# Batch 0 of an attention and mixer kernel: query and key sums, a convolution tap, u's low parts and two weight loads change engine or place

## The chip, the cores and the metric

The kernel runs on one core of one Trainium2 chip. A core has five engines with queues of their own: TensorE (PE; its weight loads are listed as PEld), VectorE (DVE), ScalarE (ACT), GpSimd (POOL) and SyncE (SP), which issues the transfers here. The metric is device microseconds of one execution.

## The reference

Four batches of 576 positions by 512 channels go through three blocks, all in f32. Only what matters here is shown:

```python
# attention, 8 heads of 64
q_d, k_d, v_d = q, k, v averaged over 4 neighbouring positions
out_up = np.repeat(sm_attn(q_d, k_d, v_d), 4, axis=2)
mask = np.abs(pos[:, None] - pos[None, :]) < 4
x = out_up + softmax(np.where(mask, scale * q @ k.T, -1e9)) @ v
# gated block: a causal depthwise convolution of 5 taps sets the gate
gate = sigmoid(sum over k of conv_w[k] * xp[:, k:k + S, :])
x = (gate * (x @ w_val)) @ w_out
# mixer: over the positions, then over the channels
u = x + (relu(x.T @ w_tok1) @ w_tok2).T
out = u + relu(u @ w_ch1) @ w_ch2
```

## The kernel before

**The attention** (`attention`, a generator per batch) treats two heads at a time, so a batch has four head pairs. For one pair, `load` brings q and k (`qk_sb`), the rows of v in groups of four (`v4_sb`) and v's windows (`v_sb`). `sums` adds groups of four of q and k into `qk_d` (line 266, a DVE reduction; for the first pair of batch 0 four accumulating PE products with a unit matrix, line 263, and an ACT copy, line 264) and groups of v on GpSimd into `vd` (lines 268, 269). `low_scores` makes the averaged scores `sc_d` (line 279) and `loc_scores` those of the band, `sc_l` (lines 319, 325). `softmax` takes maxima on DVE (line 228), exponentials on ACT (line 234) into `e_d` or `e_l`, a reciprocal on DVE (line 238) and the scaling on GpSimd (line 239). `low_turn`, `loc_turn`, `low_out` and `loc_out` transpose these and multiply with v. The averaged part is written into x by ACT (line 309) and the band's part added by DVE (line 360, "the addition" below). `conv` makes the gate from x on DVE: the first tap (line 364) is a multiplication by a scalar, the other four (line 367) multiply and add. Batch 0 takes pair i's scores two steps ahead of pair i-2's outputs.

**The weights** come as 64-bit words. `decode` turns a piece of 256 columns into f32 with three DVE instructions (lines 124, 125, 127, tile `wa`), and splits it into a high part (ACT, line 130) and a low part (GpSimd, line 131). All large products are then three PE products: high by high, high by low, low by high (lines 194 to 196). The data they meet are split alike by `hi_lo` (line 438 on ACT, line 439 on DVE or GpSimd).

**The products of a batch** (`p1`): `p_val` from x, times the gate into `y` (line 476); `p_x`, y by w_out, copied to `u_sb` (line 489); transposes of u (`x2_ps`, split in lines 499 and 500); `r_ps`, the first product over positions, and `p_h`, the second, which is added to u (line 553) and split into `u_hl` (line 554 calls `hi_lo`). `c1` multiplies `u_hl` with w_ch1 (`g_ps`), and `c2` the result with w_ch2 (`p_o`).

**The order.** Batch 0's attention comes first, its steps mixed with eight steps of loading w_val and w_out (two pieces each) and with products of zeros ("fillers", `idle_ps`, line 108). After that PE's order is the written one: `mix` runs the products of the batches one after the other and, at the places that `T_AT` (weights over positions) and `A_AT` (attention of batches 1 to 3) give in a running count of PE time, steps of other generators between them. The other engines are ordered by the framework's scheduler.

```python
T_AT = (2, 14)
A_AT = {1: (0, 57), 2: (59, 136), 3: (138, 216)}
...
    busy(NW0)
    mix((1 for _ in a[0]), [(w, 8, V0, V1), ((busy(NW1) for _ in range(21)), 21, 0, 21)])
```

Buffers that come up below: weights in 64 bits and `wa` have three each, `w_hl` (w_ch1's pieces) four, `v4` one.

Of the kernel before, what the change touches and what calls it, by code (L numbers as in the profile page):

```python
# [14 lines left out]
AF = mybir.ActivationFunctionType  # L15
ALU = mybir.AluOpType
# [18 lines left out]
TAPS = 5  # L35
# [1 line left out]
NW = 16  # L37
LAG = 2
NE = 4
T_AT = (2, 14)  # L40
C2_AT = 285
NM = 2
NW1R = 4
# [9 lines left out]
NW0, NW1 = 8, 3  # L53
# [12 lines left out]
NWD = 3  # L66
NX2 = 4
V0, V1 = 2, 22
A_AT = {1: (0, 57), 2: (59, 136), 3: (138, 216)}
W2_AT = (262, 312)  # L70
NEG = -8.0e9

# [2 lines left out]
def kernel(ctx, tc, qk, vw, v4, w_val, conv_w, w_out, w_tok1, w_tok2, w_ch1, w_ch2, out):  # L75
    nc = tc.nc
# [5 lines left out]
    def T(p, shape, dt, tag, bufs, name=None):  # L82
        return p.tile(shape, dt, tag=tag, bufs=bufs, name=name or tag)
# [15 lines left out]
    cw = T(sb, [128, KC, TAPS], F32, "cw", 1)  # L99
# [5 lines left out]
    def busy(n):  # L105
        for _ in range(n):
            p = T(ps, [128, 512], F32, "ao", BANKS["ao"], name="idle_ps")
            nc.tensor.matmul(p, lhsT=idle[:, 0:128], rhs=idle, start=True, stop=True)
# [93 lines left out]
    def load(b, hp):  # L202

        early = b == 0 and hp > 1
        t = T(sb, [128, 2, PADW], F32, "uhl" if early else "qk", NUH if early else 2, name="qk_sb")
        nc.sync.dma_start(out=t, in_=qk[b, hp])
        tag, bufs = ("x2r", NX2) if b == 0 and hp > 0 else ("v4", NV4)
        w = T(sb, [72, 4, 2, 128], F32, tag, bufs, name="v4_sb")
        nc.sync.dma_start(out=w, in_=v4[b, hp])
        return {"qk": t, "v4": w, "v": load_v(b, hp) if b == 0 else None}  # L210

    def load_v(b, hp):
        tag, bufs = ("w1", NW1R) if b == 0 and hp > 1 else ("v", NV)
        v = T(sb, [128, NCK // 2, 128], F32, tag, bufs, name="v_sb")
        nc.sync.dma_start(out=v, in_=vw[b, hp])
        return v
# [24 lines left out]
    def attention(b):  # L241
# [5 lines left out]
        def bank(shape, name):  # L247
            if b:
                tag = "as" if name[:2] == "sc" else "ao"
            else:  # L250
                tag = TAG0.get(name, "ao")
            return T(ps, shape, F32, tag, BANKS[tag], name=name)

        def sums(hp):
            d = hpd[hp]
            w = d.pop("v4")
            qk_d = T(sb, [128, 2, SD], F32, "qkd", ND, name="qk_d")
            qd, kd = qk_d[:, 0], qk_d[:, 1]
            qk_4 = d["qk"][:, :, 3:3 + S].rearrange("p i (a r) -> p i a r", r=4)
            if b + hp == 0:  # L260
                p = bank([128, 2, SD], "qk_d")
                for r in range(4):
                    nc.tensor.matmul(p, lhsT=ident, rhs=qk_4[:, :, :, r], start=(r == 0), stop=(r == 3))
                nc.scalar.activation(out=qk_d, in_=p, func=AF.Copy)
            else:
                nc.vector.tensor_reduce(out=qk_d, in_=qk_4, axis=AX.X, op=ALU.add)
            vd = d["vd"] = T(sb, [72, 2, 128], F32, "vd", NVD, name="vd")
            nc.gpsimd.tensor_tensor(out=w[:, 0:2], in0=w[:, 0:2], in1=w[:, 2:4], op=ALU.add)
            nc.gpsimd.tensor_tensor(out=vd, in0=w[:, 0], in1=w[:, 1], op=ALU.add)
            d["qkd"] = qd, kd  # L270

        def low_scores(hp):
            d = hpd[hp]
            qd, kd = d.pop("qkd")
            parts = [bank([72, 2, SD], "sc_d") for _ in range(2)]
            for c in range(2):
                for h, p in enumerate(parts):
                    r0 = 64 * h
                    nc.tensor.matmul(p[:, c, :], lhsT=qd[r0:r0 + 64, c * HD:c * HD + HD],
                                     rhs=kd[r0:r0 + 64, :], start=True, stop=True)  # L280
            e = d["ed"] = T(sb, [72, 4, SD], F32, "e", NE, name="e_d")
            softmax(parts, e, 0.125 / 16.0)
# [29 lines left out]
        def loc_scores(hp):  # L312
            d = hpd[hp]
            qk = d.pop("qk")
            parts = []
            for c0, c1 in LU:
                n = c1 - c0
                p = bank([128, n, WIN], "sc_l")
                nc.tensor.matmul(p.rearrange("p a w -> p (a w)"), lhsT=ident16,
                                 rhs=mask[:, c0:c1, :].rearrange("p a w -> p (a w)"), start=True, stop=False)  # L320
                for c in range(n):
                    o = CQ * (c0 + c)
                    for h in range(2):
                        r0 = 64 * h
                        nc.tensor.matmul(p[r0:r0 + 64, c, :], lhsT=qk[r0:r0 + 64, 0, 3 + o:3 + o + WIN],  # L325
                                         rhs=qk[r0:r0 + 64, 1, o:o + WIN], start=False, stop=(c == n - 1))
                parts.append(p)
            e = d["el"] = T(sb, [128, NCK, WIN], F32, "e", NE, name="e_l")
            softmax(parts, e, 0.125)
# [31 lines left out]

        def conv(hp, s0=0, s1=S):
            x, g = x_t[hp], g_t[hp]
            nc.vector.tensor_scalar(g[:, s0:s1], x[:, s0:s1], cw[:, hp, TAPS - 1:TAPS], None, ALU.mult)
            for sh in range(1, TAPS):
                k, t0 = TAPS - 1 - sh, max(s0, sh)
                nc.vector.scalar_tensor_tensor(out=g[:, t0:s1], in0=x[:, t0 - sh:s1 - sh], scalar=cw[:, hp, k:k + 1],  # L367
                                               in1=g[:, t0:s1], op0=ALU.mult, op1=ALU.add)
# [38 lines left out]
        for hp in range(NHP + L):  # L407
            if hp < NHP:
                if hp == 0:
                    for i in range(NHP):  # L410
                        hpd[i] = load(b, i)
                sums(hp)
                low_scores(hp)
                yield
                loc_scores(hp)
                yield
            if hp >= L:
                low_turn(hp - L)
                low_out(hp - L)
                yield  # L420
                loc_turn(hp - L)
                loc_out(hp - L)
                yield
                if hp == NHP + L - 1:
                    conv(hp - L, 0, HS)
                    sigmoid(0, HS)
                    conv(hp - L, HS, S)
                else:
                    conv(hp - L)
                yield  # L430
# [6 lines left out]
    def hi_lo(src_ap, hi_ap, lo_ap, lo_eng):  # L437
        nc.scalar.activation(out=hi_ap, in_=src_ap, func=AF.Copy)  # L438
        lo_eng.tensor_tensor(out=lo_ap, in0=src_ap, in1=hi_ap.bitcast(F32), op=ALU.subtract)  # L439
# [5 lines left out]
    def hv(hs):  # L445
        return slice(hs * HS, hs * HS + HS)
# [11 lines left out]
    def p1(b):  # L458
# [43 lines left out]
        x = x_pair(0)  # L502
# [4 lines left out]
        x = x_pair(1)  # L507
# [35 lines left out]
        us = []  # L543
        for hs in range(2):
            us.append(pair("u", "uhl", NUH))
            for c in range(KC):
                p = bank(P1T["p_h"], "p_h")
                for m in range(2):
                    mm3(p[:, 0:HS], [r[m][:, j, c * 128:c * 128 + 128] for j in range(2)],
                        [t2[m][j][:, hv(hs)] for j in range(2)], m == 0, m == 1)  # L550
                uu = u[:, c, hv(hs)]
                with first():
                    nc.vector.tensor_tensor(out=uu, in0=p[:, 0:HS], in1=uu, op=ALU.add)
                hi_lo(uu, us[hs][0][:, c], us[hs][1][:, c], nc.vector)
                if c == KC - 1:
                    c0 = b * S + hs * HS
                    nc.sync.dma_start(out=u_dr[:, :, c0:c0 + HS], in_=u[:, :, hv(hs)])
                    if hs:
                        u_hl[b] = us
                yield 6 * MM  # L560
# [86 lines left out]
    def mix(main_g, side):  # L647

        now, done = 0.0, [0] * len(side)
        for us in main_g:  # L650
            now += us
            for j, (g, n, t0, t1) in enumerate(side):
                want = n if now >= t1 else max(0, int((now - t0) * n / (t1 - t0)))
                while done[j] < want:
                    done[j] += 1
                    next(g, None)
        for g, _, _, _ in side:
            run(g)

    decode(conv_w, KC * TAPS, 128, None, None, full=cw.rearrange("p c k -> p (c k)"))  # L660
    a = [attention(b) for b in range(B)]
    w = chain(w_sq("val", w_val), w_sq("out", w_out))
    busy(NW0)
    mix((1 for _ in a[0]), [(w, 8, V0, V1), ((busy(NW1) for _ in range(21)), 21, 0, 21)])
    side = [(chain(w_t1(), w_t2()), 7, *T_AT)]
    side += [(a[b], NA, *A_AT[b]) for b in range(1, B)]
    last = c2()
# [47 lines left out]
```

## Time and profile before

| | |
|---|---|
| median of 3 runs | 672.69 us (669.57 to 675.57) |
| profiled execution | 671.3 us, of which the span is 669.5 us |
| busy in the span: PE, PEld | 617.8 us (92%), 531.7 us |
| DVE, ACT, POOL | 351.2 us (52%), 313.1 us, 185.6 us |
| mean granted TensorE clock | 0.956 of full speed |

The times of the runs cover the whole execution; the profiled span begins with its first instruction on an engine. Busy shares are means over the span, whose beginning and end differ much; the rows below therefore cut it into stretches.

### The profile page before, as it was taken

The page shows a single profiled execution, that of the slowest core. Times are in us where ns is not written, and L with a number is a line of the kernel's source. Part 1 is how long each engine was busy: PE and PEld are TensorE (multiplying, and loading weights), DVE is VectorE, ACT ScalarE, POOL GpSimd, SP SyncE. Part 2 cuts the span into 40 slices and gives each one's busy share as a digit, 9 for nine tenths or more (in the row PEclk, how much of TensorE's full clock was granted, in tenths as well). Part 3 has the DMA queues.
Part 4 walks back from the last instruction along what each step waited for, and adds up shares of the span by engine and source line. Part 5 has one row for each costly group of instructions (what it writes and reads, how often), then busy time and mean ns, then how long its engine had stood idle before and what let it go on. Part 6 is the DMA issues. An engine that isn't in the chain of part 4 may idle for free.

```text
span 669.5 us, 12775 instructions
## 1 busy us (share of the span) xinstructions
PE 617.8 (92%) x4884; PEld 531.7 (79%) x4887; DVE 351.2 (52%) x670; ACT 313.1 (47%) x1036; POOL 185.6 (28%) x210
## 2 busy tenths in 40 slices
PE   8898749779879999999999999999998999999996
PEld 4544639658778988899898999998997888888886
DVE  3889997866684456643343644107625232323232
ACT  2785357456537666645656753324433222222221
POOL 5856453431536422223331103303422000000000
PEclk9797859798898999999999999999999999999999
DMA  8634146542675344684332486565997354554220
GB/s 272 207 100 127 56 131 182 158 154 93 207 258 164 118 137 137 195 253 151 101 88 70 135 239 207 163 194 188 309 324 247 95 159 157 156 160 126 79 76 33
DMA packets 53901, 107.23 MB, mean 160 GB/s; under 512 B 5776, under 2 KB 21392, under 8 KB 53840
## 3 DMA queue, kind: packets, MB, share of 16 engines
q1 hardware_dynamic: 53840, 106.42, 51.1%
q8 instruction: 38, 0.62, 0.4%
q14 instruction: 23, 0.19, 0.1%
HBM read 76.52 MB, written 29.88 MB: 159 GB/s over the span
## 4 chain that ended last, share of the span: by engine, by line
PE 59%; DVE 6%; DMA 5%; ACT 3%; issue 2%; POOL 1%; SPq 0%; DVEq 0%; ACTq 0%; POOLq 0%
PE p_o L194 7%; PE p_o L196 7%; PE p_o L195 7%; PE g_ps L194 5%; PE g_ps L195 4%; PE g_ps L196 4%; DMA w<-in_w_ch_dram 4%; PE p_x L194 2%; PE sc_l L325 2%; PE p_val L194 2%; PE p_val L195 2%; PE p_val L196 2%; PE p_x L196 2%; PE p_x L195 2%; PE r_ps L194 1%
## 5 line engine op out<-in xcount | busy, mean ns | idle before, releaser
L194 PE MATMUL g_ps<-u_hl,w_hl 128*128 128x288 f32 x384 | 117.1, 305 | 1.7 <-ACT u_hl L438 1.7
L195 PE MATMUL g_ps<-u_hl,w_hl 128*128 128x288 f32 x384 | 113.9, 297 | 0.3 <-DVE u_hl L439 0.2
L196 PE MATMUL g_ps<-u_hl,w_hl 128*128 128x288 f32 x384 | 113.3, 295 | 0.0
L194 PE MATMUL p_o<-g_hl,ch 128*128 128x512 f32 (+1 forms) x240 | 89.3, 372 | 1.9 <-ACT r_sb L580 1.9
L439 DVE TENSOR_TENSOR g_hl<-r_back,g_hl 128x512 fp32r<-128x512 f32 (+1 forms) x60 | 39.4, 656 | 96.8 <-ACT g_hl L438 91.1
L195 PE MATMUL p_o<-g_hl,ch 128*128 128x512 f32 (+1 forms) x240 | 89.1, 371 | 0.0
L196 PE MATMUL p_o<-g_hl,ch 128*128 128x512 f32 (+1 forms) x240 | 89.1, 371 | 0.0
L438 ACT ACTIVATE g_hl<-r_back 128x512 fp32r<-128x512 f32 (+1 forms) x60 | 35.3, 589 | 110.7 <-PE p_o L196 108.3
L194 PEld LDWEIGHTS g_ps<-u_hl,w_hl 128*128 128x128 f32 x384 | 72.6, 189 | 4.9 <-ACT u_hl L438 1.9
L195 PEld LDWEIGHTS g_ps<-u_hl,w_hl 128*128 128x128 f32 x384 | 72.7, 189 | 0.7 <-DVE u_hl L439 0.7
L196 PEld LDWEIGHTS g_ps<-u_hl,w_hl 128*128 128x128 f32 x384 | 72.7, 189 | 0.0
L367 DVE SCALAR_TENSOR_TENSOR gate_sb<-x_f,cw,gate_sb 128x575 f32<-128x575 f32 (+5 forms) x68 | 60.9, 900 | 0.8
L580 ACT ACTIVATE r_sb<-g_ps 128x288 f32<-128x288 f32 x96 | 38.4, 406 | 48.0 <-PE g_ps L196 40.3
L124 DVE TENSOR_SCALAR wa<-w 128x256 int32<-128x256 int32 (+2 forms) x76 | 39.3, 524 | 35.3 <-DMA w<-in_w_ch_dram 23.7
L194 PEld LDWEIGHTS p_o<-g_hl,ch 128*128 128x128 f32 x240 | 45.2, 188 | 10.9 <-ACT r_sb L580 2.7
L196 PEld LDWEIGHTS p_o<-g_hl,ch 128*128 128x128 f32 x240 | 45.2, 188 | 8.3
L195 PEld LDWEIGHTS p_o<-g_hl,ch 128*128 128x128 f32 x240 | 45.2, 188 | 8.2
L234 ACT ACTIVATE e_l<-sc_l,mx 128x64 f32<-128x64 f32 x160 | 48.2, 334 | 0.4
L194 PE MATMUL p_val<-x_hl,val_hi 128*128 128x288 f32 x128 | 40.7, 318 | 5.8 <-DVE y L476 4.4
L194 PE MATMUL p_x<-y_hl,out_hi 128*128 128x288 f32 x128 | 41.5, 325 | 2.3 <-ACT u_sb L489 1.6
L195 PE MATMUL p_x<-y_hl,out_hi 128*128 128x288 f32 x128 | 39.6, 309 | 2.9 <-DVE y_hl L439 2.8
L439 POOL TENSOR_TENSOR x_hl<-x_f,x_hl 128x288 fp32r<-128x288 f32 x32 | 26.2, 830 | 54.3 <-ACT x_hl L438 54.3
(107 smaller groups left out, 1347.4 us busy)
## 6 DMA issues: line engine op xcount, KB each, us to landing
w_hl<-w_dr SPq DMA_DIRECT2D x36, 512.0 KB
r_dr<-r_sb SPq DMA_DIRECT2D x48, 288.0 KB
w<-in_w_ch_dram SPq DMA_DIRECT2D x48, 256.0 KB
r_back<-r_dr SPq DMA_DIRECT2D x48, 256.0 KB
qk_sb<-in_qk_dram SPq DMA_DIRECT2D x16, 589.0 KB
w_dr<-w_hl SPq DMA_DIRECT2D x12, 512.0 KB
v_sb<-in_vw_dram SPq DMA_DIRECT2D x16, 320.0 KB
v_sb<-in_v_dram SPq DMA_DIRECT2D x16, 288.0 KB
```

The source lines that it names most:

```text
L124: nc.vector.tensor_scalar(a, high, 3, 0x3FFFFFF8, ALU.logical_shift_left, ALU.bitwise_and)
L194: nc.tensor.matmul(out_ap, lhsT=lh, rhs=rh, start=first, stop=False)
L195: nc.tensor.matmul(out_ap, lhsT=lh, rhs=rl, start=False, stop=False)
L196: nc.tensor.matmul(out_ap, lhsT=ll, rhs=rh, start=False, stop=last)
L234: nc.scalar.activation(out=e[:, o, :], in_=p[:, c, :], func=AF.Exp, scale=scale, bias=mx[:, o:o + 1], accum_out=sm[:, o:o + 1])
L325: nc.tensor.matmul(p[r0:r0 + 64, c, :], lhsT=qk[r0:r0 + 64, 0, 3 + o:3 + o + WIN], rhs=qk[r0:r0 + 64, 1, o:o + WIN], start=False, stop=(c ...
L367: nc.vector.scalar_tensor_tensor(out=g[:, t0:s1], in0=x[:, t0 - sh:s1 - sh], scalar=cw[:, hp, k:k + 1], in1=g[:, t0:s1], op0=ALU.mult, op1 ...
L438: nc.scalar.activation(out=hi_ap, in_=src_ap, func=AF.Copy)
L439: lo_eng.tensor_tensor(out=lo_ap, in0=src_ap, in1=hi_ap.bitcast(F32), op=ALU.subtract)
L580: nc.scalar.activation(out=r[:, hv(hs)], in_=p[:, 0:HS], func=AF.Relu)
```

## The change

In batch 0, the sums of q and k of all four pairs are made as the first pair's are (PE products and an ACT copy). The first tap of batch 0's convolution is made by ACT. Batch 0's generator stops once after two of its four pairs' loads, and two steps (four pieces) of w_val are issued there; the other six steps stay in the mix. The low part of u is made by GpSimd in all batches. Two places in the running count change: the weights over positions end later, and batch 1's attention runs from 8 to 59 in place of 0 to 57.

```diff
-T_AT = (2, 14)
+T_AT = (2, 20)
...
-A_AT = {1: (0, 57), 2: (59, 136), 3: (138, 216)}
+A_AT = {1: (8, 59), 2: (59, 136), 3: (138, 216)}
...
-            if b + hp == 0:
+            if b == 0:
                 p = bank([128, 2, SD], "qk_d")
...
-            nc.vector.tensor_scalar(g[:, s0:s1], x[:, s0:s1], cw[:, hp, TAPS - 1:TAPS], None, ALU.mult)
+            if b:
+                nc.vector.tensor_scalar(g[:, s0:s1], x[:, s0:s1], cw[:, hp, TAPS - 1:TAPS], None, ALU.mult)
+            else:
+                nc.scalar.activation(out=g[:, s0:s1], in_=x[:, s0:s1], func=AF.Copy, scale=cw[:, hp, TAPS - 1:TAPS])
...
                         hpd[i] = load(b, i)
+                        if i == 1:
+                            yield
...
-                hi_lo(uu, us[hs][0][:, c], us[hs][1][:, c], nc.vector)
+                hi_lo(uu, us[hs][0][:, c], us[hs][1][:, c], nc.gpsimd)
...
-    mix((1 for _ in a[0]), [(w, 8, V0, V1), ((busy(NW1) for _ in range(21)), 21, 0, 21)])
+    next(a[0])
+    for _ in range(2):
+        next(w)
+    mix((1 for _ in a[0]), [(w, 6, V0, V1), ((busy(NW1) for _ in range(21)), 21, 0, 21)])
```

The first place is DVE's start in batch 0. `sc_l` and `sc_d` are the scores, `mx` their maxima, `qk_d` the sums. Before:

```order
L266 TENSOR_REDUCE qk_d<-qk_sb 128x288
L228 TENSOR_REDUCE mx<-sc_l 128x6
L228 TENSOR_REDUCE mx<-sc_d 72x2 x2
L228 TENSOR_REDUCE mx<-sc_l 128x4
L266 TENSOR_REDUCE qk_d<-qk_sb 128x288
```

After the change, DVE at the same place (`wa` and `w_138`, `w_146`, `w_156` are three pieces of w_val):

```order
L124 TENSOR_SCALAR wa<-w_138 128x256
L125 SCALAR_TENSOR_TENSOR wa<-w_138,wa 128x256
L127 SCALAR_TENSOR_TENSOR wa<-w_138,wa 128x256
L124 TENSOR_SCALAR wa<-w_146 128x256
L125 SCALAR_TENSOR_TENSOR wa<-w_146,wa 128x256
L124 TENSOR_SCALAR wa<-w_156 128x256
L127 SCALAR_TENSOR_TENSOR wa<-w_146,wa 128x256
L125 SCALAR_TENSOR_TENSOR wa<-w_156,wa 128x256
L228 TENSOR_REDUCE mx<-sc_l 128x6
```

Eight instructions on weights now stand ahead of the first maximum, and the sums are gone from the queue.

The second place is PE's written order where batch 1's first head pair has given its scores, among the products of batch 0. Before (`out3` and `out0` are parts of w_out):

```order
L319 MATMUL sc_l_1137<-mask_70,ident16_68 128x256
L325 MATMUL sc_l_1137<-qk_sb_1004 64x64 x8
L279 MATMUL sc_d_1177<-qk_d_1170 72x144
L279 MATMUL sc_d_1178<-qk_d_1170 72x144
L279 MATMUL sc_d_1177<-qk_d_1170 72x144
L279 MATMUL sc_d_1178<-qk_d_1170 72x144
L194 MATMUL p_x2_1095<-y_hl_961,out3_hi_930 128x288
```

After the change, from the same scores on (the `p_val` group has twelve such rows, three for each of four parts of w_val, and `sc_d` follows behind them):

```order
L319 MATMUL sc_l_1214<-mask_70,ident16_68 128x256
L325 MATMUL sc_l_1214<-qk_sb_1136 64x64 x8
L501 MATMUL x2_ps_1243<-ident_63,u_sb_966 128x128 x4
L194 MATMUL p_val_1251<-x_hl_1055,val0_hi_136 128x288
L195 MATMUL p_val_1251<-x_hl_1055,val0_hi_136 128x288
L196 MATMUL p_val_1251<-x_hl_1055,val0_lo_137 128x288
```

Four transposes and twelve products now stand between one pair's band scores and the next pair's averaged scores, which stood back to back before.

The third place is GpSimd's queue while batch 1's `p_h` runs; `e_d`, `e_l`, `v4_sb` and `vd` belong to the attention of batch 3. Before:

```order
L239 TENSOR_TENSOR e_d_3257<-e_d_3257,sm_3259 72x576
L269 TENSOR_TENSOR vd_3853<-v4_sb_3813 72x256
L239 TENSOR_TENSOR e_l_3359<-e_l_3359,sm_3361 128x640
L268 TENSOR_TENSOR v4_sb_3981<-v4_sb_3981 72x512
L439 TENSOR_TENSOR x_hl_3776<-x_f32_2427,x_hl_3776 128x288
```

After the change:

```order
L444 TENSOR_TENSOR u_hl_3314<-u_sb_2395,u_hl_3314 128x288 x2
L239 TENSOR_TENSOR e_d_3272<-e_d_3272,sm_3274 72x576
L269 TENSOR_TENSOR vd_3868<-v4_sb_3828 72x256
L444 TENSOR_TENSOR u_hl_3314<-u_sb_2395,u_hl_3314 128x288 x2
L239 TENSOR_TENSOR e_l_3374<-e_l_3374,sm_3376 128x640
L444 TENSOR_TENSOR u_hl_3436<-u_sb_2395,u_hl_3436 128x288 x2
L268 TENSOR_TENSOR v4_sb_3996<-v4_sb_3996 72x512
L444 TENSOR_TENSOR u_hl_3436<-u_sb_2395,u_hl_3436 128x288 x2
```

The eight low parts of u stand between the attention's instructions, the last two behind the sum of `v4_sb` (line 268).

## Rows read from the trace of the kernel before

**Rows 1.** Stretches: us, busy PE, PEld, DVE, ACT, POOL (instructions), clock, DMA share, GB/s.

```profile
9.94:20.00 10.06, 10.00 (x102) 5.61 (x101) 6.88 (x11) 5.99 (x37) 5.31 (x6) 1.00 1.03 313
20.00:38.56 18.56, 16.15 (x158) 9.66 (x158) 16.55 (x36) 14.06 (x75) 13.30 (x12) 0.72 0.49 170
38.56:71.42 32.86, 26.82 (x259) 14.77 (x261) 30.01 (x51) 18.62 (x67) 21.73 (x22) 0.89 0.37 109
71.42:116.27 44.85, 32.63 (x303) 29.15 (x302) 39.81 (x89) 26.91 (x107) 19.01 (x24) 0.77 0.42 124
116.27:163.94 47.67, 37.22 (x314) 30.92 (x309) 34.99 (x66) 24.84 (x78) 13.81 (x15) 0.86 0.42 129
163.94:205.29 41.35, 34.24 (x305) 31.53 (x303) 29.14 (x59) 19.67 (x66) 17.36 (x20) 0.92 0.72 240
205.29:669.50 464.21, 453.12 (x3442) 406.54 (x3442) 192.40 (x358) 201.77 (x607) 89.14 (x98) 1.00 0.51 158
```

**Rows 2.** PE's waits, 71.42 to 205.29 us: total us, times, longest.

```profile
PE sc_l L319 <- ACT e_d L234: 7.5, 2, 5.8
PE sc_d L279 <- ACT e_l L234: 6.4, 2, 5.9
PE p_val L194 <- DVE y L476: 4.4, 1, 4.4
PE r_ps L195 <- DVE x_hl L500: 2.8, 1, 2.8
```

**Rows 3.** DVE's groups by shape, 0 to 205.29 us: busy us, mean ns, idle before.

```profile
L124 DVE TENSOR_SCALAR wa<-w 128x256 int32<-128x256 int32 x46 | 28.4, 627 | 12.7 <-POOL w_hl L131 7.7 <-DMA w<-in_w_ch_dram 2.8 <-POOL val_lo L131 1.3
L125 DVE SCALAR_TENSOR_TENSOR wa<-w,wa 128x256 int32<-128x256 int32 x46 | 25.1, 556 | 0.3
L127 DVE SCALAR_TENSOR_TENSOR wa<-w,wa 128x256 int32<-128x256 int32 x46 | 21.9, 485 | 0.3
L266 DVE TENSOR_REDUCE qk_d<-qk_sb 128x288 f32<-128x1152 f32 x9 | 12.1, 1348 | 11.4 <-DMA qk_sb<-in_qk_dram 11.4
L439 DVE TENSOR_TENSOR u_hl<-u_sb,u_hl 128x288 fp32r<-128x288 f32 x8 | 4.4, 566 | 3.6 <-ACT u_hl L438 3.6
L364 DVE TENSOR_SCALAR gate_sb<-x_f,cw 128x576 f32<-128x576 f32 x7 | 4.1, 579 | 0.0
L364 DVE TENSOR_SCALAR gate_sb<-x_f,cw 128x288 f32<-128x288 f32 x2 | 0.6, 357 | 0.0
```

**Rows 4.** PE's sums of the first head pair, the same view.

```profile
L263 PE MATMUL qk_d<-qk_sb,ident 128*128 128x288 f32 x8 | 4.4, 704 | 1.2 <-DMA qk_sb<-in_qk_dram 1.2
```

**Rows 5.** ACT's copies into x, the same view.

```profile
L309 ACT ACTIVATE x_f<-o_d 128x576 f32<-128x576 f32 x8 | 5.2, 656 | 3.6 <-PE o_d L306 3.5
```

**Rows 6.** Transfers of one head pair: KB each.

```profile
qk_sb<-in_qk_dram SPq DMA_DIRECT2D x16, 589.0 KB
v_sb<-in_vw_dram SPq DMA_DIRECT2D x16, 320.0 KB
v_sb<-in_v_dram SPq DMA_DIRECT2D x16, 288.0 KB
```

**Rows 7.** DVE in time: start, us, instruction, idle before and its releaser.

```profile
12.43 0.56 DVE L228 TENSOR_REDUCE mx<-sc_l 128x6 f32<-128x384 f32 x1 [1.14 <-PE sc_l L325]
...
21.03 1.31 DVE L124 TENSOR_SCALAR wa<-w 128x256 int32<-128x256 int32 x1 [0.57 <-DMA w<-in_w_val_dram]
...
38.56 0.83 DVE L360 TENSOR_TENSOR x_f<-o_l,x_f 128x290 f32<-128x290 f32 x2 [0.50 <-PE o_l L354]
...
68.33 0.81 DVE L360 TENSOR_TENSOR x_f<-o_l,x_f 128x290 f32<-128x290 f32 x2
```

**Rows 8.** GpSimd's low parts of x by shape, whole span.

```profile
L439 POOL TENSOR_TENSOR x_hl<-x_f,x_hl 128x288 fp32r<-128x288 f32 x32 | 26.2, 830 | 54.3 <-ACT x_hl L438 54.3
```

**Rows 9.** GpSimd while batch 1's p_h runs, in time.

```profile
280.65 1.28 POOL L268 TENSOR_TENSOR v_sb<-v_sb 72x512 f32<-72x512 f32 x1 [0.20 <-DMA v_sb<-in_v_dram]
```

**Rows 10.** One slow instruction of DVE, and GpSimd's scaling beside it, in time.

```profile
119.20 2.90 DVE L124 TENSOR_SCALAR wa<-w 128x256 int32<-128x256 int32 x1 [0.89 <-DMA w<-in_w_ch_dram]
120.68 1.26 POOL L239 TENSOR_TENSOR e_l<-e_l,sm 128x640 f32<-128x640 f32 x1
```

## The prediction

> **What bounds the kernel now.** I read the stretches first [rows 1]. Behind 205.3 us PE is busy 453.1 of 464.2 us at full clock: only PE's own work counts there, and the change leaves that as it is. What can be won lies ahead. PE stands idle for 44.9 - 32.6 = 12.2 us between 71.4 and 116.3, for 10.5 in the next stretch and for 7.1 in the one behind, and its granted clock in these is 0.77, 0.86 and 0.92, so that a part of each passed at 1.2 in place of 2.4 GHz. DVE is the busiest engine of the first two but for PE: 39.8 of 44.9 us and 35.0 of 47.7. Up to 71.4 us batch 0's attention and the weights share DVE and ACT; PE also runs the products of zeros there, so that its busy share says little of need.
>
> Then PE's waits [rows 2]: 5.8 us for the exponentials of `e_d` and 5.9 for those of `e_l`, both of batch 1's first pairs; 2.8 for DVE's split of the transposes, 4.4 for `y`. The releaser of the two long ones is ACT, but ACT waits for maxima, and those stand in DVE's queue among pieces of weights, as DVE's load shows. I read what ends last in these stretches as DVE's backlog.
>
> The sum is made against the profiled execution, 671.3 us (a span of 669.5 and 1.8 around it); the median of the runs, 672.7, is 1.4 us above.
>
> **Stage 1, to 71.4 us.** Removed from DVE: three sums of 1.348 us, 4.0 us, and the first taps, 3 x 0.579 + 2 x 0.357 = 2.5 us [rows 3]. They go to PE, where one pair's sums took 4.4 us [rows 4], 13.2 us for three, and to ACT as three copies and five taps. ACT's price for these isn't in the trace; a copy into x of twice a copy's size took 0.66 us [rows 5], so eight cost at most 5.3. From 9.9 to 71.4 us ACT was busy 38.7 of 61.5 us and PE 53.0 [rows 1], an idle time of 22.8 and of 8.5: on ACT the work has room, on PE part of it has.
>
> Some weights come earlier. The loads of two pairs, 2 x 1.197 MB [rows 6], no longer stand ahead of the first piece; at 313 GB/s [rows 1] that is 7.6 us, so the piece that DVE began at 21.03 [rows 7] comes at about 13.4. Eight instructions on weights now stand ahead of the first maximum: three of 0.627, three of 0.556 and two of 0.485 us [rows 3], 4.5 us. The maximum that began at 12.43 [rows 7] begins at some 17.9, 5.5 us later, and batch 0's chain of scores, exponentials and outputs hangs on it. Against that stand the 4.0 us of sums that DVE no longer makes on the way to the first addition. I count half, since ACT and PE are in that chain too: the first addition moves from 38.56 [rows 7] by 5.5 - 2.0 = 3.5 us. Bounds: 0, if all relief tells and the weights that are done early are missing from the queue later; 8, if the two later pairs arrive late as well.
>
> From the first addition to the last (68.33 [rows 7]) DVE gets one and a quarter pieces more, at 0.627 + 0.556 + 0.485 = 1.67 us 2.1 us, and two sums of batch 1, 2.7, that stood ahead before, less three taps, 1.7: 3.1 us more. DVE was idle for 2.9 us from 38.6 to 71.4 [rows 1], which I let take half: 1.6. The stage ends 5.1 us later, within 0 and 9. **+5**.
>
> **Stage 2, to 116.3 us.** Here the earlier weights pay. By the last addition DVE has done the rest of w_out and much of the first weights over positions, about six pieces more than before: 6 x 1.67 = 10.0 us that leave its 39.8. PE's order now also has four transposes and twelve products between the first pair's band scores and the next `sc_d`. The next stretch has 314 of PE's instructions in 37.2 us [rows 1], 0.12 each, so they cover some 1.9 us of the 5.9 us wait. Cover and relief together I let take the two long waits from 11.8 to 6.8 us: a gain of 5. The clock of 0.77 means that nearly half of the stretch passed at the lower level; with PE standing still less I let it come to 0.87, what the next stretch has: 32.6 x (1 - 0.77/0.87) = 3.8 us. Least: the cover and half the relief's share, 4. Most: all 12.2 us of idle time and a little clock, 13. **-9**.
>
> **Stage 3, to 163.9 us.** The low parts of u leave DVE, 8 x 0.566 = 4.5 us [rows 3], and five pieces of w_ch1 are already done, 8.4 us; DVE's 35.0 us [rows 1] become 22. The wait for the split of the transposes, 2.8 [rows 2], and others like it lose their ground; of 10.5 us of idle time I leave 5, a gain of 5.5. With the clock from 0.86 to 0.92 (the stretch behind) there are 37.2 x (1 - 0.86/0.92) = 2.4 us more. On GpSimd a low part of this size took 0.83 us [rows 8] against DVE's 0.57: the last of eight is ready 0.3 us later. Least 3 (half the waits), most 13 (all of both). **-8**.
>
> **Stage 4, to 205.3 us.** PE's 4.4 us for `y` [rows 2] stand at the end of a stretch in which DVE decodes w_ch1, makes batch 1's convolutions and waits for buffers: 7.7 us of `wa`'s idle time went to GpSimd's low parts of `w_hl` [rows 3]. None of that is removed, and pieces that are done earlier also hold their four buffers earlier. **0**, within -4 and 4.
>
> **Stage 5.** Batches 1 to 3 give 24 more low parts to GpSimd, 19.9 us on an engine that is busy 89.1 of 464.2 us [rows 1, 8]. But its queue is one. In batch 1 the last two low parts stand behind the sum of `v4_sb`, which began at 280.65, when its transfer had come [rows 9], and which itself waits on low parts now; behind it the two end at 281.9 + 2 x 0.83 = 283.6, later by what the transfer is late. They would hold `g_ps` of batch 1 by little or nothing. **+1**, within 0 and 4; there is no gain, since PE is busy all along.
>
> **The sum** is 5 - 9 - 8 + 0 + 1 = -11: 660.3 us against the profiled 671.3, 661.7 on the scale of the median. I predict 661.
>
> **A rule that speaks against the change.** One instruction of line 124 took 2.90 us at 119.20 where the group's mean is 0.63, and lies over GpSimd's scaling of `e_l`, 120.68 to 121.94 [rows 3, 10]. The Trainium skill (SBUF — State Buffer, "Who interferes with whom") says that GpSimd reading SBUF and a DVE instruction that has two inputs there, or that runs in a mode with two ports, lock each other out for a whole instruction. By that rule each low part that moves to GpSimd can hold up a DVE instruction; the trace agrees in this pair of rows. What it would give here is rival D.
>
> **The rivals.**
>
> (B) DVE bounds to 163.9 us as before. For it: DVE is busy 89% and 73% of stages 2 and 3 [rows 1], and w_ch1's pieces wait in line, so that each gap may be filled with the next piece while the maxima wait as now. Then only what is removed counts, 4.0 + 2.5 + 4.5 = 11 us, of which I let 8 reach the end, less the 5 of the later start: -3, 668, or 669 on the median's scale. Against it: PE's order gives cover that doesn't depend on DVE.
>
> (D) The low parts on GpSimd block DVE. In stage 3 eight of 0.83 us [rows 8] hold up 6.6 us of an engine that is needed for the additions to u: -11 + 6.6, 667, or 668. For it speaks the 2.90 us [rows 10]; against it that DVE has little else to do there once five pieces are gone.
>
> (C) Slower: PE becomes the bound of stage 1. Its queue is in order, and the sums of three pairs stand in it among the scores and outputs of the pairs before. From 20 to 38.6 us its clock was 0.72 [rows 1]. At the lower level three sums take 3 x 8.8 = 26.4 us; less the 8.5 us in which PE was idle that is 17.9, without it 26.4. Such a delay of all that follows gives 661.7 + 17.9 = 680, up to 688. The point from which it decides: a stage 1 that ends over 16 us later (5 and the 11 that the forecast gains) is slower than before. Against it: the stage's products of zeros need no result, and the first sums ran at clock 1.00 or near it [rows 1, 4].
>
> **How the numbers follow.** The forecast has 0.60: 0.54 of it faster by over 1%, which is about what a measurement of this kernel can tell from no change (below 666.0 us), 0.06 within. B has 0.18 (0.05 and 0.13), D 0.10 (0.03 and 0.07), C 0.12 (0.10 slower, 0.02 within). Together: faster 0.62, same 0.28, slower 0.10. The half-widths of the terms, 4.5, 4.5, 5, 4 and 2, make 9 us if they are independent of each other; the clock, which is in two of them, joins their low ends, so the range reaches 13 below: low 648. Above, it takes in B and D and ends short of C: high 676.
>
> **What would show it.** Right: the first maximum at 17 to 18 us; batch 0's last addition at 72 to 75; behind it no wait of PE over 4.5 us for `e_d` or `e_l`; the first `g_ps` at about 152 in place of 163.9; and from there to the end the same time. Stage 1 is wrong if the last addition comes at 80 or later, with PE's sums ahead of what it waits for. B would show the same two waits of nearly 6 us, D decoding instructions of over 1.5 us beside `u_hl` on GpSimd, a wrong stage 5 waits of `g_ps` for GpSimd's `u_hl`. What I can't see is where the clock falls next: if it falls as often as now, its 6 us are lost and the time is 667.

## The result, and the profile after

The changed kernel takes 665.73 us (median of 11 runs, 664.11 to 668.48) against 672.21 us of the kernel before beside it: a ratio of 0.9904, 95% interval 0.9879 to 0.9928. That is 6.5 us faster, where 11 were forecast. The profiled execution took 664.67 us (span 662.8) against 671.3 (669.5), 6.6 less.

The stretches of the kernel after answer to [rows 1]. They are cut at the same events: the first addition, the point from which `p_val` runs steadily, the end of batch 0's `p_val` (115.60 us in the kernel before, in place of the 116.27 of [rows 1]), the first `g_ps`, the end of batch 1's first 48 `p_val` (207.03 before). Columns as in [rows 1].

```profile
20.00:45.17 25.17, 23.07 (x196) 10.92 (x194) 15.93 (x36) 18.60 (x104) 16.07 (x17) 1.00 0.62 195
45.17:80.08 34.91, 29.82 (x284) 16.28 (x282) 32.84 (x55) 21.69 (x75) 19.40 (x21) 0.90 0.33 93
80.08:113.32 33.24, 26.47 (x209) 23.35 (x209) 31.66 (x75) 20.52 (x77) 15.71 (x18) 0.95 0.45 140
113.32:151.11 37.79, 35.12 (x353) 30.02 (x352) 29.62 (x53) 23.93 (x89) 15.32 (x16) 0.91 0.49 153
151.11:201.20 50.09, 40.63 (x368) 36.57 (x367) 33.47 (x64) 26.97 (x83) 26.18 (x29) 0.86 0.58 195
201.20:662.80 461.60, 449.50 (x3431) 404.74 (x3429) 185.90 (x332) 200.02 (x605) 105.25 (x121) 1.00 0.51 160
```

The same stretches of the kernel before, cut at its events:

```profile
71.42:115.60 44.18, 31.96 (x267) 28.55 (x267) 39.36 (x88) 26.25 (x105) 18.67 (x23) 0.77 0.41 122
115.60:163.94 48.34, 37.89 (x349) 31.53 (x349) 35.45 (x66) 25.50 (x81) 14.15 (x15) 0.86 0.43 131
163.94:207.03 43.09, 35.98 (x318) 33.27 (x317) 29.96 (x60) 20.84 (x68) 18.73 (x22) 0.92 0.71 237
207.03:669.50 462.47, 451.38 (x3431) 404.80 (x3429) 191.59 (x356) 200.60 (x605) 87.77 (x97) 1.00 0.51 158
```

| stage | before | after | difference | forecast |
|---|---|---|---|---|
| 1, to steady `p_val` | 71.42 | 80.08 | +8.7 | +5 |
| 2 | 44.18 | 33.24 | -10.9 | -9 |
| 3 | 48.34 | 37.79 | -10.6 | -8 |
| 4 | 43.09 | 50.09 | +7.0 | 0 |
| 5 | 462.47 | 461.60 | -0.9 | +1 |

Up to the first `g_ps` 12.8 us are won, and 7.0 of them are gone 50 us later; most of these 7.0 are products that stood before the first `g_ps` and now stand behind it, as shown below. PE's waits from 140 to 215 us after the change, which answer to [rows 2] (total, times, longest):

```profile
PE o_l L354 <- ACT pts_l L343: 3.6, 1, 3.6
PE sc_l L319 <- ACT e_d L234: 2.6, 1, 2.6
PE g_ps L195 <- POOL u_hl L444: 1.6, 3, 0.8
```

The 4.4 us for `y` are no longer there. A wait of 3.6 us for ACT's copies of the transposes stands in their place. In stages 2 and 3 the two waits of nearly 6 us are gone. From 80.08 to 151.11 us these are left of them (the longest anywhere is now the 2.6 above, in stage 4):

```profile
PE sc_l L319 <- ACT e_d L234: 2.2, 1, 2.2
PE sc_d L279 <- ACT e_l L234: 1.0, 1, 1.0
```

DVE in time, for [rows 7] (start, us, idle before):

```profile
16.19 0.55 DVE L228 TENSOR_REDUCE mx<-sc_l 128x6 f32<-128x384 f32 x1
...
45.17 0.83 DVE L360 TENSOR_TENSOR x_f<-o_l,x_f 128x290 f32<-128x290 f32 x2 [2.69 <-PE o_l L354]
...
77.01 0.81 DVE L360 TENSOR_TENSOR x_f<-o_l,x_f 128x290 f32<-128x290 f32 x2
```

The first maximum is 3.8 us later than before, the first addition 6.6 and the last 8.7. Each of these times is from one execution. sig_before, a kernel below whose edit leaves batch 0 alone, has the first addition at 41.16 and the last at 73.70 in its one profile (of the slowest of its runs), 2.6 and 5.4 us later than the kernel before. So differences of a few us in batch 0 count here only where several kernels agree.

### The profile page after: what moved, and what is told of

It reads as the page before. It is cut to its first block, busy times and chain, and to the rows that moved or that the text cites. A ratio compares the mean times of both kernels' runs of the same rounds, so it can differ in the third digit from the quotient of the medians.

```text
span 662.8 us, 12825 instructions
## 1 busy us (share of the span) xinstructions
PE 622.3 (94%) x4911; PEld 529.6 (80%) x4911; DVE 339.4 (51%) x630; ACT 316.4 (48%) x1044; POOL 210.0 (32%) x242
## 4 chain that ended last, share of the span: by engine, by line
PE 60%; DVE 6%; DMA 5%; ACT 3%; issue 2%; POOL 1%; SPq 0%; DVEq 0%; ACTq 0%
PE p_o L194 7%; PE p_o L196 7%; PE p_o L195 7%; PE g_ps L194 5%; PE g_ps L195 5%; PE g_ps L196 5%; DMA w<-in_w_ch_dram 4%; PE sc_l L325 2%; PE p_x L194 2%; DVE wa L124 2%; PE p_x L195 2%; PE p_x L196 2%; PE p_val L194 2%; PE p_val L196 2%; PE p_val L195 2%
## 5 line engine op out<-in xcount | busy, mean ns | idle before, releaser
L370 DVE SCALAR_TENSOR_TENSOR gate_sb<-x_f,cw,gate_sb 128x575 f32<-128x575 f32 (+5 forms) x68 | 62.8, 930 | 1.5 <-ACT gate_sb L367 0.5
L124 DVE TENSOR_SCALAR wa<-w 128x256 int32<-128x256 int32 (+2 forms) x76 | 37.1, 499 | 34.8 <-DMA w<-in_w_ch_dram 21.1
L194 PE MATMUL p_x<-y_hl,out_hi 128*128 128x288 f32 x128 | 40.9, 320 | 4.2 <-ACT u_sb L494 3.7
L125 DVE SCALAR_TENSOR_TENSOR wa<-w,wa 128x256 int32<-128x256 int32 (+2 forms) x76 | 44.2, 591 | 1.1
L444 POOL TENSOR_TENSOR x_hl<-x_f,x_hl 128x288 fp32r<-128x288 f32 x32 | 27.7, 877 | 45.5 <-ACT x_hl L443 44.8
```

The costliest lines, as they stand in the source:

```text
L124: nc.vector.tensor_scalar(a, high, 3, 0x3FFFFFF8, ALU.logical_shift_left, ALU.bitwise_and)
L125: nc.vector.scalar_tensor_tensor(out=a, in0=high, scalar=-0x40000000, in1=a, op0=ALU.bitwise_and, op1=ALU.bitwise_or)
L194: nc.tensor.matmul(out_ap, lhsT=lh, rhs=rh, start=first, stop=False)
```

## The experiments

Ratios are to the kernel before, run beside it on the same chip, with 95% intervals; the change has 0.9904 (0.9879 to 0.9928). All start from the change or from the kernel before and take out or put in one part or two. The parts add lines, so the same statement has line numbers that differ by a few from kernel to kernel.

**Taking one part out of the change.** u's low parts back on DVE:

```diff
-                hi_lo(uu, us[hs][0][:, c], us[hs][1][:, c], nc.gpsimd)
+                hi_lo(uu, us[hs][0][:, c], us[hs][1][:, c], nc.vector)
```

> The change without its part on u: all low parts of u stay on DVE. The first theory (DVE's backlog sets the stretch up to the first g_ps, so its relief pays) expects 4.5 us of DVE back in batch 0's p_h stretch and 668 to 670 us against 665.7 of the change. The second theory (read from the trace of the change: GpSimd's eight low parts hold g_ps by 1.6 us and, through ACT's in-order wait for g_ps, the exponentials of e_d near 158 us) expects 662 to 664 us.

0.9900 (0.9870 to 0.9931): no difference, so neither theory holds. The first `g_ps` comes at 154.2 in place of 151.1 us, but the wait for `u_hl` is no shorter with DVE's low parts (1.9 us) than with GpSimd's (1.6), and the end is the same.

The sums of pairs 1 to 3 back on DVE:

```diff
-            if b == 0:
+            if b + hp == 0:
```

> The change with the sums of q and k of batch 0's pairs 1 to 3 back on DVE. First theory (DVE relief): 4.0 us of DVE come back on batch 0's chain, half of it reaches the end, 667 to 669 us. Second theory (PE's queue: 3.3 us of the last pair's sums stand between the first pair's output products from 41.2 us on): the first addition comes at about 42 us in place of 45.2, and the time is 662 to 664 us.

0.9942 (0.9911 to 0.9973). The first addition came at 42.0 us, as the second theory said, the last at 77.7, no earlier than the change's 77.0. The median, 668.4 us, is in the first theory's range, but the interval overlaps the change's, so a loss is likely and not shown.

The first tap back on DVE:

```diff
-            if b:
+            if True:
                 nc.vector.tensor_scalar(g[:, s0:s1], x[:, s0:s1], ...
```

> The change with batch 0's first tap back on DVE. First theory: 2.5 us of DVE come back, 667 to 668 us. Second theory (ACT has room and DVE isn't what ends last at the taps): within 1 us of the change, 665 to 666.5 us.

0.9944 (0.9912 to 0.9976), 666.95 us, between the two theories' ranges; this interval overlaps the change's too. The last addition came at 79.3.

The loads in one go again, and all weights in the mix:

```diff
-                        if i == 1:
-                            yield
...
-    next(a[0])
-    for _ in range(2):
-        next(w)
-    mix((1 for _ in a[0]), [(w, 6, V0, V1), ...
+    mix((1 for _ in a[0]), [(w, 8, V0, V1), ...
```

> The change with all four pairs' loads ahead of the weights again, and eight weight steps in the mix. First theory (the early pieces carry stage 2's and 3's gain): batch 0 starts 4 us earlier but stages 2 and 3 lose about 9, 669 to 672 us. Second theory (PE's new order around batch 1's scores carries the gain, the early pieces only delay batch 0): 662 to 664 us.

0.9980 (0.9949 to 1.0010): the gain is gone, as the first theory said. But its reason for the delay of batch 0 fell: the first maximum came at 12.85 us, and the last addition still at 78.1. What delays batch 0 in the change isn't the early weights.

The places as before:

```diff
-T_AT = (2, 20)
-A_AT = {1: (8, 59), 2: (59, 136), 3: (138, 216)}
+T_AT = (2, 14)
+A_AT = {1: (0, 57), 2: (59, 136), 3: (138, 216)}
```

> The change with the places of the weights over positions and of batch 1's attention as before. First theory (the early weights carry the gain, the new places only add cover): the two waits for e_d and e_l come back in part, 667 to 669 us against 665.7 of the change. Second theory (the new order of PE around batch 1's scores carries most of it): 670 to 672 us, as before the change. Third theory (batch 0 ends 9 us later because batch 1's first pair now starts later or stands otherwise): the last addition of batch 0 at about 70 in place of 77 us.

0.9945 (0.9916 to 0.9973), which overlaps the change's interval as well; the median, 669.65 us, stands at the border of the first two theories. The last addition came at 77.7, so the third fell. So four single parts taken out left the last addition between 77.7 and 79.3, and the fifth, u's, at 77.8.

**Two parts put into the kernel before**, the early weights and the new places, with nothing else:

```diff
-T_AT = (2, 14)
+T_AT = (2, 20)
...
-A_AT = {1: (0, 57), ...
+A_AT = {1: (8, 59), ...
...
                         hpd[i] = load(b, i)
+                        if i == 1:
+                            yield
...
-    mix((1 for _ in a[0]), [(w, 8, V0, V1), ...
+    next(a[0])
+    for _ in range(2):
+        next(w)
+    mix((1 for _ in a[0]), [(w, 6, V0, V1), ...
```

> The kernel before with two parts of the change alone: the early weights and the new places of batch 1's attention and of the weights over positions; sums, tap and u's low parts as before. First theory (these two carry the gain): 665 to 668 us against 672 of the kernel before. Second theory (they pay only where DVE is freed of sums and taps): 669 to 672 us.

0.9806 (0.9763 to 0.9848), 660.73 us: twice the gain of the whole change, more than either theory had. The last addition comes at 71.35 us. Its stretches behind batch 0:

```profile
74.80:107.34 32.54, 25.93 (x209) 23.03 (x209) 31.03 (x68) 19.59 (x74) 14.06 (x18) 0.95 0.31 93
107.34:147.84 40.50, 34.38 (x354) 28.08 (x352) 36.16 (x71) 25.86 (x95) 18.28 (x18) 0.96 0.61 199
147.84:197.52 49.68, 40.38 (x368) 37.01 (x367) 34.90 (x68) 27.14 (x83) 19.25 (x22) 0.86 0.60 198
```

Stages 2 and 4 are those of the change within 0.7 us; stage 3 is 2.7 us longer; what is better, by about 5, is stage 1. That pointed to the sums, the tap or u's low parts as what costs the change its batch 0.

**One part added to these two.** The sums, then the tap, then u's low parts, each by its lines of the change's diff.

> Early weights and new places alone (early_spread, 0.981 of the kernel before), plus the sums of batch 0 on TensorE. First theory (the sums in PE's queue are what the whole change loses in batch 0: its first addition came at 45.2 us with them and at 39.9 in early_spread): first addition at 44 to 46, last at 75 to 78 in place of 72.2, ratio 0.988 to 0.992. Second theory (no part alone does it, DVE's relief makes up for it): ratio 0.979 to 0.983, as early_spread.

0.9912 (0.9882 to 0.9943), first addition 45.1, last 77.3 us: the first theory. PE there (start, us):

```profile
38.02 0.56 PE L354 MATMUL o_l<-pts_l,v_sb 64*64 64x58 f32 x12
...
41.12 3.29 PE L263 MATMUL qk_d<-qk_sb,ident 128*128 128x288 f32 x6
44.34 0.79 PE L354 MATMUL o_l<-pts_l,v_sb 64*64 64x58 f32 x28
```

The last pair's sums, with six fillers ahead of them, stand between the two halves of the first pair's output, for which the addition waits. In early_spread the last of that output stands at

```profile
39.13 0.70 PE L354 MATMUL o_l<-pts_l,v_sb 64*64 64x58 f32 x16
```

> early_spread plus batch 0's first tap on ACT. First theory (the tap is free on ACT and relieves DVE a little): ratio 0.977 to 0.982, as early_spread or a little faster. Second theory (ACT's queue is in order, and a tap or a sigmoid that waits for DVE's taps holds up what is behind it, the copies of the last pair's transposes): last addition of batch 0 later by 2 to 5 us than in early_spread, ratio 0.985 to 0.990.

0.9933 (0.9906 to 0.9961), last addition 77.8 us: the second theory, and more than it had. The profile is of the slowest of its runs (674.1 us against a median of 667.3), so only its part up to 78 us is read. ACT there, and then in early_spread:

```profile
62.78 0.43 ACT L443 ACTIVATE x_hl<-x_f 128x288 fp32r<-128x288 f32 x1
68.72 0.44 ACT L375 ACTIVATE gate_sb<-gate_sb 128x288 f32<-128x288 f32 x1 [5.51 <-DVE gate_sb L370]
69.07 0.39 ACT L295 ACTIVATE pts_d<-pt_d 72x288 f32<-72x288 f32 x1
```

```profile
60.57 0.78 ACT L372 ACTIVATE gate_sb<-gate_sb 128x288 f32<-128x288 f32 x2 [0.17 <-DVE gate_sb L367]
64.61 0.89 ACT L295 ACTIVATE pts_d<-pt_d 72x288 f32<-72x288 f32 x2 [3.27 <-PE pt_d L292]
```

With the tap on ACT, a sigmoid stands idle for 5.5 us until DVE's other taps of that gate are done, and the copies of the last pair's transposes (`pts_d`) are behind it: 69.07 in place of 64.61. DVE's taps are late, first of all because the first one now is. The addition of that pair was done at 56.4 us; ACT made the tap from 58.14, behind a table load and another sigmoid, and DVE, whose queue is in order, had three pieces of weights ahead of the second tap, which it began at 62.34. In early_spread DVE began the same tap at 56.21, after an addition done at 55.3. Besides, the third tap took 3.08 us, where such taps took 0.80 in the kernel before (at 55.10 and 56.16). Over the same time GpSimd summed `v_sb` (62.95 to 64.28) and made two low parts of weights (to 65.65). So most of the delay is the order of the queues (6.1 us at the second tap); the rest, 2 us, is about what the slow tap lost. That GpSimd held this tap is read from the overlap alone.

The same wait of a sigmoid for DVE's taps stands ahead of `pts_d` with the sums alone (3.0 us, `pts_d` at 69.7) and in the change (3.5 us, `pts_d` at 69.2). That fits that the two parts don't add: last addition 77.3 with the sums, 77.8 with the tap, 77.0 with both. All nine kernels here with either part, the change and its variants among them, end batch 0 between 77.0 and 79.3, and the three with the early weights and neither part (early_spread, es_u, es_sig) between 71.4 and 72.9.

> early_spread plus u's low parts on GpSimd in all batches. First theory (no gain and no loss: undoing it in the change gave the same ratio): 0.979 to 0.983. Second theory (it relieves DVE in the stretch up to the first g_ps by 4.5 us, which reaches the end where batch 0 isn't late): 0.974 to 0.978. Third theory (GpSimd and DVE block each other or GpSimd's queue holds g_ps): 0.984 to 0.988.

0.9827 (0.9797 to 0.9857), 660.84 us: the first theory, no gain and no loss.

**The sigmoids held back**, to see what takes 7 us in stage 4. ACT after the change:

```profile
154.50 0.21 ACT L230 ACTIVATE mx<-mx 72x4 f32<-72x4 f32 x1 [0.16 <-DVE mx L228]
154.72 1.28 ACT L375 ACT_TABLE_LOAD   x1
156.01 0.69 ACT L375 ACTIVATE gate_sb<-gate_sb 128x576 f32<-128x576 f32 x1
158.16 0.41 ACT L585 ACTIVATE r_sb<-g_ps 128x288 f32<-128x288 f32 x1 [1.46 <-PE g_ps L196]
158.59 1.28 ACT L234 ACT_TABLE_LOAD   x1
159.89 0.38 ACT L234 ACTIVATE e_d<-sc_d,mx 72x144 f32<-72x144 f32 x1
...
184.04 0.42 ACT L130 ACTIVATE w_hl<-wa 128x256 fp32r<-128x256 f32 x1 [3.12 <-DVE wa L127]
184.47 1.28 ACT L375 ACT_TABLE_LOAD   x1
185.77 0.68 ACT L375 ACTIVATE gate_sb<-gate_sb 128x576 f32<-128x576 f32 x1
186.36 0.39 ACT L585 ACTIVATE r_sb<-g_ps 128x288 f32<-128x288 f32 x1
186.65 0.76 ACT L343 ACTIVATE pts_l<-pt_l 128x384 f32<-128x384 f32 x2
```

The maxima are ready at 154.7, but the exponentials begin at 159.89: a sigmoid with its table, a copy that waits for `g_ps`, and the exponential's table stand between. The copies `pts_l`, whose transposes were done by 182.0, stand behind a split of weights that waited for DVE until 184.04, and behind a table and a sigmoid. The edit gives the sigmoids of batches 1 to 3 a bias of zero that is made from the last pair's gate (in es_sig from its x, which is there a convolution sooner):

```diff
+            z = 0.0
+            if b:
+                z = T(sb, [128, 1], F32, "zero", 2, name="zero")
+                nc.vector.tensor_scalar(z, g_t[-1][:, S - 1:S], 0.0, None, ALU.mult)
             for g in g_t:
-                nc.scalar.activation(out=g[:, s0:s1], in_=g[:, s0:s1], func=AF.Sigmoid)
+                nc.scalar.activation(out=g[:, s0:s1], in_=g[:, s0:s1], func=AF.Sigmoid, bias=z)
```

> The change, with the sigmoids of batches 1 to 3 held until the last pair's convolution is done (they get a bias of zero that is computed from it; the result is the same). In the change ACT loads the sigmoid's table at 154.7 us, a moment before the maxima are there, and at 184.5 us. If these hops give back what was won up to the first g_ps: PE's waits of 2.6 us for e_d and of 3.6 us for pts_l go, 661 to 663 us. If the pairs' chain is bound elsewhere (weights' buffers, DVE): 665 to 667 us, the same as the change.

0.9850 (0.9801 to 0.9900) with the hold put into the change. The interval overlaps the change's own, so a gain is likely and not shown. The wait for `pts_l` went and that for `e_d` fell to 1.3 us, but one of 5.3 us for `y` came, behind the held sigmoids, the first of which began at 194.25.

> The kernel before with the same hold on the sigmoids of batches 1 to 3. If the hops cost only where PE comes early, as in the change: within 1.5 us of the kernel before, 671 to 673 us. If they hold batch 1's attention in any order: 667 to 669 us.

0.9919 (0.9884 to 0.9954) with the hold put into the kernel before: 5.4 us, as the second theory said, so the hops cost there too. Where, is open: in the one profile, the two waits for `e_d` and `e_l` are still 5.8 and 5.9 us, and the stretch from the last addition to the first `g_ps` takes 90.0 us in place of 95.6.

> early_spread with the sigmoids of batches 1 to 3 held until the last pair's addition is done (not its convolution, so that three of four are out of the way when y needs them). If the sigmoid hops in front of the exponentials and of pts_l (waits of 2.6 and 3.6 us of PE) hold the end: these waits go, a wait for y of 1 to 3 us comes, and the ratio is 0.973 to 0.977. If the pairs' chain is bound by DVE's decoding there: 0.979 to 0.983.

0.9781 (0.9748 to 0.9814) on early_spread, 658.03 us: the fastest kernel of the study. Its interval overlaps that of early_spread (0.9806), so the hold is not shown to pay there. PE's waits from 140 to 215 us:

```profile
PE pt_d L292 <- DVE x_f L360: 3.3, 1, 3.3
PE p_val L194 <- DVE y L482: 2.3, 1, 2.3
```

`pts_l` no longer holds PE, and `e_d` only for 0.3 us; DVE's additions and `y` do. The ratio lies between the ranges of its two stories.

## Why the prediction was right in sum, and where its steps were not

**Direction and range held**: -6.5 us on the medians, forecast -11 in a range of 648 to 676. By the number alone rival B, 669 on the median's scale, was nearer than the forecast's 661. What tells them apart is the trace: B's sign, the same two waits of nearly 6 us, isn't there.

**Stages 2 and 3: right in sum and in kind.** Together 17 us were foreseen and 21.5 came, of which 4.6 are the piece that left stage 3 (see stage 4), so 16.9. The split between the two isn't tested, because stage 2 also handed 58 products on (267 before, 209 after). The early weights and PE's order carry the gain. From the last addition to the first `g_ps` it took 95.6 us before and 74.1 in the change, 76.5 with the two parts alone, 81.0 with the early weights taken out and 82.9 with the places as before. The first `g_ps` was foreseen at 152 and came at 151.1 us. That the maxima waited behind weights in DVE's queue, and no longer do, shows at batch 1's first pair. Before, the first of its `sc_l` were done at 88.9 us and their maximum began 3.2 us later, behind an instruction on weights of 1.97 us (line 125, from 89.31); after, they were done at 101.65 and DVE had waited for them (one row before, one after):

```profile
92.06 0.54 DVE L228 TENSOR_REDUCE mx<-sc_l 128x6 f32<-128x384 f32 x1
```

```profile
101.69 0.56 DVE L228 TENSOR_REDUCE mx<-sc_l 128x6 f32<-128x384 f32 x1 [0.33 <-PE sc_l L325]
```

Whether one of the two alone would do without the other parts was not run. The sizes inside were rougher: 19 pieces of weights were done by the last addition in place of 14, five more where six were foreseen; the clock of stage 2 came to 0.95 and not 0.87; and DVE's 35 us of stage 3 became 29.6, not 22. So less of stage 3's gain can be relief of DVE than was foreseen.

**Stage 1 is where the forecast failed**: "Against that stand the 4.0 us of sums that DVE no longer makes ... I count half", and "on ACT the work has room". Both moves were booked as relief or as free. Each alone costs: 0.9912 and 0.9933 against 0.9806, with intervals apart, 5.7 and 6.5 us on the medians. Spare time of an engine, 22.8 us on ACT, was the wrong measure; its instructions run in the order of its queue, and what stood behind the moved work was on the path. The first addition came 6.6 us later where 3.5 were foreseen. For the sums this is rival C in kind (PE's queue in order) but not at its price: the sums ran at full clock there (3.29 us for six of eight products, the stretch's clock 1.00), and the stage ended 8.7 us later, not 16. The start that I took for the reason of the lateness, the eight decoding instructions, cost 3.8 us at the first maximum and little at the last addition: early_spread has them too and ends batch 0 at 71.4, between the 68.3 and 73.7 of the two kernels that load as before and have neither part; and the change without them has its first maximum at 12.85 and still ends batch 0 at 78.1.

**u's low parts: mis-sized.** "The low parts of u leave DVE, 8 x 0.566 = 4.5 us" was right in the trace and worth nothing: 0.9827 with them and 0.9806 without, 0.9904 and 0.9900. DVE was idle for 7.4 us from 155.4 after the change, so that it had no use for the time:

```profile
162.77 0.56 DVE L228 TENSOR_REDUCE mx<-sc_l 128x6 f32<-128x384 f32 x1 [7.41 <-PE sc_l L325]
```

Rival D, that GpSimd's low parts block DVE, is out at its price of 6.6 us by the same two pairs. In single rows it shows. The 2.90 us of [rows 10] lay over three instructions of GpSimd in a row (118.75 to 121.94), not over the scaling alone. After the change, beside u's low parts, taps of 0.80 us took 0.99, 0.99 and 0.97 (at 149.80, 151.08 and 154.39). GpSimd's other work does more: the tap of 3.08 us in es_tap, and after the change DVE's tap of 1.54 us at 177.38 beside GpSimd's sum of `v_sb` from 177.13 to 178.61. In that last case the trace agrees with the Trainium skill (SBUF — State Buffer, "Who interferes with whom"). But the three decoding instructions together took 0.500 + 0.641 + 0.542 = 1.68 us in the mean up to 201 us, as against 1.67 before [rows 3].

**Stage 4: 0 forecast, +7.0 measured**, and nearly all of it is work that changed stage. The last pair's `sc_l` of batch 1 with its wait, and eight transposes, stood before the first `g_ps` and now stand behind it. In the kernel before:

```profile
156.14 0.93 PE L292 MATMUL pt_d<-ident,e_d 72*72 72x72 f32 x8
...
160.32 0.32 PE L319 MATMUL sc_l<-mask,ident 128*128 128x384 bf16 x1 [1.63 <-ACT e_d L234]
...
161.63 0.68 PE L325 MATMUL sc_l<-qk_sb 64*64 64x64 f32 x16
```

and after the change:

```profile
153.14 0.66 PE L292 MATMUL pt_d<-ident,e_d 72*72 72x72 f32 x8
160.76 0.48 PE L319 MATMUL sc_l<-mask,ident 128*128 128x384 bf16 x1 [2.64 <-ACT e_d L234]
...
162.98 1.12 PE L325 MATMUL sc_l<-qk_sb 64*64 64x64 f32 x16
```

Before, that is 0.93 + 1.63 + 1.99 = 4.55 us of stage 3; after, 0.66 + 2.64 + 3.34 = 6.64 of stage 4, because the products run at the lower clock level behind the wait (the granted clock was 0.57 from 158 to 166 us, and 1.00 from 158 to 164 before the change). With the piece put back, stage 4 lost 0.4 (0 foreseen), and the piece itself costs 2.1 more. So PE came 12.8 us earlier to the first `g_ps`, but the exponentials of `e_d` began at 159.9 in place of 159.4: ACT's chain was no earlier. The 3.6 us wait for `pts_l` later on stands where 4.4 for `y` stood.

**Stage 5**: +1 foreseen, -0.9 measured. The last two low parts of batch 1 ended at 279.0 us, and `g_ps` waited 0.4 us for GpSimd in all.

In the profiled executions the forecast of the sum is off by 4.3 us (-6.7 against -11), its terms by 17 when taken one by one: stages 1 and 4 were worse by 3.7 and 7.0, stages 2, 3 and 5 better by 1.9, 2.6 and 1.9. Some of that is where the border of stages 3 and 4 lies; that the rest partly cancels is luck.

## What to carry to other kernels

Idle time of an engine does not say that moved work is free: look for what stands behind it in that engine's queue, and what that holds. When a change has several parts, try them apart. Here two of five gave 1.9%, two others took half of it back and the fifth did nothing, and taking single parts out would not have shown it, since each of two parts alone already brings the whole loss. When stages are cut at an event of one engine, look at what has changed sides before calling the time won or lost: here 4.6 us left one stage and came back as 6.6 in the next.

## What the runs showed of the hardware

A change of table on ACT took 1.28 us each time, 19 of them in either kernel besides the first, and each stands in ACT's queue in front of what comes next. The instruction behind a load began 1.30 us after the load began (158.59 to 159.89). The Trainium skill (ScalarE: Activation LUTs, "What ACT_TABLE_LOAD costs") has the same 1283 ns for the load, and a drain of about 1380 ns beside it; in these rows the load alone is seen.
